# Wider idle matmuls and merged memsets at the start of a sliding-window attention and MLP kernel

## The chip, the cores and the metric

The kernel runs on one core of a Trainium2 chip. The metric is the device time of one execution in microseconds (us); lower is better. TensorE (PE) does matrix products and writes them to PSUM, VectorE (DVE), ScalarE (ACT) and GpSimd (POOL) work on data in SBUF and PSUM, and transfers are issued from GpSimd, ScalarE and SyncE (SP).

## What is computed

Windowed attention (each query sees the keys at most 32 positions away) over 8 batches of 8 heads, 576 tokens and 64 dimensions, and then an MLP with a squared ReLU on the 4608 tokens that come out.

```python
def _attn_ref(q, k, v):                      # each (8, 8, 576, 64)
    scores = scale * np.matmul(q, k.transpose(0, 1, 3, 2))
    mask = np.abs(pos[:, None] - pos[None, :]) <= 32
    scores = np.where(mask, scores, -1000000000.0)
    scores = scores - np.max(scores, axis=-1, keepdims=True)
    attn = np.exp(scores)
    attn = attn / (np.sum(attn, axis=-1, keepdims=True) + 1e-09)
    return np.matmul(attn, v)

def _moe_ref(x, w_in, w_out):                # x (4608, 512), w_in (512, 2048)
    r = np.maximum(x @ w_in, 0.0)
    return (r * r) @ w_out
```

## The kernel before

Every piece of work is recorded as an operation with its engine, its reads and writes, an estimated duration and a key (`Prog.rec`). A planner (`schedule`, `forward`, `backward`) then simulates the engines and the transfer queues with these estimates, tries several orders, keeps the best, and writes the instructions out engine by engine in that order. Between engines, and between dependent instructions of VectorE or of ScalarE, the kernel waits on semaphores that are worked out from the reads and writes; on TensorE the order alone does it.

A batch has nine chunks of 64 queries. For a chunk, K and Q (token by token in `kraw` and `qraw`) are transposed on TensorE (`tok_turn`, line 490) and copied to `kt` and `qt` (lines 501 and 504); from the second or third batch on most transposes are done by transfers. `scores` multiplies them (line 596), ScalarE takes the exponential and VectorE multiplies by the band mask into `pt` (line 633). `av` multiplies `pt` with V (lines 739 and 740), `evac` divides by the sums (lines 750 and 752) into `xr`, `xturn` transposes that (line 768) and ScalarE copies it to `xt`. For the first two chunks the mask is instead added in PSUM by a matmul of the identity with `neg` (line 580), ahead of the scores, and `pt` comes straight from the exponential.

V lies in `vx`, with two columns of ones beside the 64 of each head, so that the product with `pt` also gives the sums. Odd chunks need V shifted by 64 rows; `vd_half` makes that copy, `vd`, on VectorE (line 542). The MLP follows: `mm1_small` in pieces of 128 tokens at first (line 787), then `mm1_half` (line 810) and `mm1` (line 828), with ReLU on ScalarE and the square on VectorE (line 843) into `gt`, and `mm2` (line 880) with the second weights. MLP work of one tile of 512 tokens is interleaved with the attention of later ones.

Two parts concern this change. First, `fill`: after planning, it goes through TensorE's operations up to the first matmul of the MLP (`self.first`) or 36 us of the plan, and puts idle matmuls into the planned gaps. These multiply a tile of zeros, `zz`, with itself into a PSUM bank, `outp1`, that nobody reads before the MLP writes it (line 411). Each has 128 columns; the planner counts 107 ns for it in the first 6 us of the plan and 54 ns after that. A gap gets as many as fit, times a factor (1.15 early, 0.95 later), and the first matmul of the MLP gets six more ahead of it.

Second, the setup on VectorE, all through `ms` (line 405). `setup_ptz` zeroes four stretches of 64 columns in each of the three parts of `pt` (12 memsets). `setup_rest` is called for both buffers of batch data. It zeroes 32 rows of `vx` at either end of the sequence, sets the columns of ones in the rows beside them and in between (four memsets), and zeroes the 32 columns of padding at either end of `kt`. `setup_masks` builds the identity, `mask` and `neg` on the same engine between them.

Of the kernel before, what the change touches and what calls it, by code (L numbers as in the profile page):

```python
# [11 lines left out]
B_, H_, S_, D_ = 8, 8, 576, 64  # L12
# [7 lines left out]
VS = D_ + 2  # L20
KW = 32 + S_ + 32
LEAD = 12
WARM, COLD, DENSE, SPARSE, EXTRA = 36000, 6000, 1.15, 0.95, 6
# [24 lines left out]
class Prog:  # L48
# [257 lines left out]
    def fill(self, out):  # L306
        at = 1200
        for op in sorted((o for o in out if o.eng == "PE"), key=lambda o: o.start):
            gap = min(op.start, WARM, self.first.start) - at
            one = 107 if at < COLD else 54  # L310
            for k in range(int((gap - 60) * (DENSE if at < COLD else SPARSE) // one) + (EXTRA if op is self.first else 0)):
                w = Op()
                w.eng, w.fn, w.dma, w.deps, w.i = "PE", self.idle, None, {self.idle_on}, op.i
                w.inc, w.val, w.sem, w.start, w.end, w.dur, w.key = False, None, None, min(at + one * k, op.start - 1), 0, one, -99
                out.append(w)
            at = max(at, op.start + op.dur)
        self.ops = sorted(out, key=lambda o: (o.start, o.i))

# [40 lines left out]
class Gen:  # L359
# [47 lines left out]
    def setup_idle(self):  # L407

        self.ms("DVE", ["zz"], self.ZZ[:], 0.0, -1000, 200)
        self.p.idle_on = self.p.ops[-1]  # L410
        self.p.idle = lambda e: e.matmul(self.OUTP[1][:, 0:128], self.ZZ[:, 0:128], self.ZZ[:, 0:128], start=True, stop=True)  # L411

    def setup_masks(self, key):
        self.p.rec("POOL", lambda e: e.iota(self.IOTA[:], [[1, 256]], base=0, channel_multiplier=-1), writes=["iota"],
# [15 lines left out]
                   reads=["iota"], writes=[("mask2", 1)], key=-20, dur=130)  # L430

    def setup_rest(self, i, key):
        for s, r in ((0, 0), (4, 96)):
            self.ms("DVE", [("vxz", i, s)], self.VX[i][r:r + 32, s, :, :], 0.0, key, 160)
        self.ms("DVE", [("vxone", i, 0)], self.VX[i][32:64, 0, :, 64:VS], 1.0, key, 80)
        self.ms("DVE", [("vxone", i, 1)], self.VX[i][64:128, 0, :, 64:VS], 1.0, key, 80)
        self.ms("DVE", [("vxone", i, 2)], self.VX[i][0:96, 4, :, 64:VS], 1.0, key, 80)
        self.ms("DVE", [("vxone", i, 3)], self.VX[i][:, 1:4, :, 64:VS], 1.0, key, 120)
        self.ms("DVE", [("ktpad", i, 0)], self.KT[i][:, :, 0:32], 0.0, key)
        self.ms("DVE", [("ktpad", i, 1)], self.KT[i][:, :, 32 + S_:KW], 0.0, key)  # L440

    def setup_ptz(self, i, key):
        for j in range(4):
            self.ms("DVE", [("ptz", i)], self.PT[:, 768 * i + 192 * j + 64:768 * i + 192 * j + 128], 0.0, key, 70)

    def pieces(self, b):
        return PIECE2 if b >= TB else PIECE if b else PIECE0
# [88 lines left out]
    def vd_half(self, b, s0, s1, key, tie=()):  # L536
        vd, vx = self.VD[b % 2], self.VX[b % 2]
        for lo in range(2):
            dst = vd[64 * lo:64 * lo + 64, s0:s1, :, :].rearrange("p s h d -> p (s h d)")
            src = vx[64 - 64 * lo:128 - 64 * lo, s0 + lo:s1 + lo, :, :].rearrange("p s h d -> p (s h d)")  # L540
            rd = list(tie) + [("vxl", b % 2, s + lo) + u for s in range(s0, s1) for u in ((), (1,))] + [("vxone", b % 2, k) for k in range(4)]
            self.p.rec("DVE", lambda e, d=dst, c=src: e.tensor_copy(d, c), reads=rd,  # L542
                       writes=[("vd", b % 2, s, lo) for s in range(s0, s1)], key=key, dur=80 + 145 * (s1 - s0), att=True)

# [10 lines left out]

    def qk_tags(self, b, c):
        i = b % 2
        rd = [("ktpad", i, 0), ("ktpad", i, 1)]
        for x, (t0, n) in enumerate(self.pieces(b)):
            if t0 < 64 * c + 96:  # L560
                rd.append(("k", i, x))
            if t0 < 64 * c + 64:
                rd.append(("q", i, x))
        return rd
# [83 lines left out]
    def v_tags(self, b, c):  # L648
        i, s = b % 2, c // 2
        if c % 2:  # L650
            return [("vd", i, s, 0), ("vd", i, s, 1)]
        return [("vxl", i, s), ("vxl", i, s, 1)] + [("vxone", i, k) for k in range(4)] + ([("vxz", i, s)] if s in (0, 4) else [])

    def av3(self, n, w):
        b, c = divmod(n, NCH)
# [66 lines left out]
    def av(self, n):  # L722
        b, c = divmod(n, NCH)
        i = b % 2
        s = c // 2
        key = n - LEAD
        vt = self.VX[i][:, s] if c % 2 == 0 else self.VD[i][:, s]
        x = n % 3
        k = self.group[n][1]
        bank = "BD"[n % 2] if n < 8 else "CB"[k] if self.group[n][2] > 1 else "B"  # L730
        tag, avp = "s" + bank, self.BK[bank]
        self.bank[n] = bank

        def f(e):
            for j in range(4):
                ha = 4 * (j // 2) + j % 2
                o = avp[:, VE * j:VE * j + VE]
                a = 768 * x + 192 * (2 * (j % 2) + j // 2)
                e.matmul(o, self.PT[:, a:a + 128], vt[:, ha, 0:VE], start=True, stop=False)
                mm = e.matmul(o, self.PT[:, a + 64:a + 192], vt[:, ha + 2, 0:VE], start=False, stop=True)  # L740
            return mm

        self.p.rec("PE", f, reads=self.v_tags(b, c) + [("pt", x), ("ptz", x)], writes=[tag], key=key, dur=240, att=True)

    def evac(self, n, m, gi, k):
        rs, y = self.RS[n % 4], gi % 4
# [167 lines left out]
    def build(self):  # L914
# [4 lines left out]
        K = -200.0  # L919
        self.setup_idle()  # L920
        self.setup_masks(K - 20)
        self.setup_rest(0, K + 3)
        self.setup_ptz(0, K + 2)
        self.setup_ptz(1, K + 2)
        self.setup_ptz(2, K + 2)
        self.setup_rest(1, -20)
        at = {it: K + 1 + k for k, it in enumerate(ORDER)}
        for d in range(4):
# [4 lines left out]
        for b in range(B_):  # L933
# [24 lines left out]
            for c in range(NCH):  # L958
                n = NCH * b + c
# [33 lines left out]
                if c % 2 and not b:  # L993
                    x = (c + 1) // 2
# [6 lines left out]
                gi, k, m = self.group[n]  # L1001
# [48 lines left out]
```

The softmax here doesn't subtract the row's maximum and nothing guards it: scores larger than these inputs give would overflow.

## Time and profile before

| | us |
|---|---|
| median of 4 runs | 300.65 |
| lowest and highest of them | 300.43, 300.88 |
| the profiled execution | 301.47 |
| its span, first to last instruction | 299.7 |

The profile is of one execution. It gives the busy time of each engine, a timeline, and a chain of waits: from the last instruction back to what released it, and so on to the start. Operations are named by output and input tile and by line, so `outp<-zz` at line 411 is an idle matmul. A matmul's own duration in the profile includes its way through the array, some 0.2 us, in which the next ones already run; the rate is read from the spacing of starts, or from the chain, where each piece ends when the next begins. `(partitions x elements, type)` gives an instruction's shape. Some matmuls can be missing from a trace.

How the page splits the span into 40 slices of 7.5 us shows where each engine is busy, in tenths, and the granted clock of TensorE:

```profile
PE   7799999999999999999999999999999999999996
...
DVE  5875646764988965886569745756477622222200
...
POOL 8999841431524544442434334234410000000000
PEclk9999999999999999999999999999999999999999
DMA  9999999999999999999999999999993110100022
```

The part of the program that the change touches is the first three slices.

### The profile page before, as it was taken

The numbers are of one execution on the slowest core, as the hardware profiler recorded it, in microseconds if no ns is written. First come the engines' busy times: TensorE is split into PE (matmuls) and PEld (weight loads), VectorE is DVE, ScalarE is ACT, GpSimd is POOL, SyncE is SP. The second block draws the span as 40 slices with busy tenths as digits, with TensorE's granted clock in tenths as the row PEclk, the third lists the DMA queues.
The fourth block names the chain that finished last, engine by engine and source line by source line (L and its number), as shares of the span: only waits on it lengthen the run. The fifth ranks groups of instructions, "written<-read, shape, count | busy, mean of one in ns | idle before, by whom it ended". The sixth has DMA issues, their size and how long they took to land.

```text
span 299.7 us, 7036 instructions
## 1 busy us (share of the span) xinstructions
PE 290.7 (97%) x2754; PEld 171.7 (57%) x2789; DVE 176.3 (59%) x428; ACT 160.2 (53%) x267; POOL 104.8 (35%) x131
## 2 busy tenths in 40 slices
PE   7799999999999999999999999999999999999996
PEld 7699955866767764545445444544444444444445
DVE  5875646764988965886569745756477622222200
ACT  3466633656757665665647554664656443444311
POOL 8999841431524544442434334234410000000000
PEclk9999999999999999999999999999999999999999
DMA  9999999999999999999999999999993110100022
GB/s 155 168 202 170 206 172 194 151 144 196 152 176 160 126 180 161 152 137 181 131 132 137 152 164 130 120 151 147 156 121 76 49 49 35 37 35 36 35 89 89
DMA packets 166817, 39.34 MB, mean 131 GB/s; under 512 B 157824, under 2 KB 162304, under 8 KB 166784
## 3 DMA queue, kind: packets, MB, share of 16 engines
q0 software_dynamic: 113120, 17.90, 89.4%
q1 hardware_dynamic: 46512, 11.15, 25.9%
q10 hardware_dynamic: 7152, 9.83, 10.1%
q8 instruction: 22, 0.36, 0.5%
q14 instruction: 11, 0.09, 0.1%
HBM read 36.70 MB, written 9.44 MB: 154 GB/s over the span
## 4 chain that ended last, share of the span: by engine, by line
PE 92%; DVE 3%; DMA 2%; issue 1%; ACT 0%; ACTq 0%; POOL 0%; DVEq 0%; POOLq 0%
PE outp L880 40%; PE ht L828 27%; PE ht L810 7%; PE ht L787 7%; PE sc L664 3%; PE sc L596 3%; DMA kraw<-in_k_dram 2%; DVE vd L542 1%; PE sc L490 1%; DVE xr L752 1%; PE sc L856 1%; PE outp L856 1%; PE outp L411 1%; PE sc L712 0%; DVE kt L504 0%
## 5 line engine op out<-in xcount | busy, mean ns | idle before, releaser
L880 PE MATMUL outp<-w,gt 128*128 128x512 bf16 x534 | 133.9, 379 | 2.0 <-issue 1.0
L843 DVE TENSOR_TENSOR gt<-rt 128x512 bf16<-128x512 bf16 x144 | 59.6, 419 | 62.8 <-ACT rt L834 53.3
L828 PE MATMUL ht<-xt,w 128*128 128x512 bf16 x375 | 95.8, 379 | 0.6 <-issue 0.2
L834 ACT ACTIVATE rt<-ht 128x512 bf16<-128x512 f32 x96 | 57.3, 599 | 68.9 <-PE ht L828 64.2
L880 PEld LDWEIGHTS outp<-w,gt 128*128 128x128 bf16 x560 | 52.4, 98 | 57.4
L828 PEld LDWEIGHTS ht<-xt,w 128*128 128x128 bf16 x384 | 36.8, 98 | 43.1
L464 POOL DMA_DIRECT2D qraw<-in_q_dram x39 | 34.1, 875 | 49.7 <-PE ht L828 13.2
L464 POOL DMA_DIRECT2D kraw<-in_k_dram x39 | 34.2, 876 | 36.8 <-PE ht L828 17.6
L530 POOL DMA_DIRECT2D vx<-in_v_dram x40 | 35.1, 879 | 29.2 <-PE ht L828 15.7
L624 ACT ACTIVATE e<-sc 128x1024 bf16<-128x1024 f32 (+1 forms) x46 | 35.7, 819 | 8.2 <-PE sc L596 8.2
L887 ACT ACTIVATE oe<-outp 128x512 f32<-128x512 f32 x35 | 20.9, 598 | 22.4 <-PE outp L880 22.4
L688 DVE TENSOR_TENSOR xr<-pf,rs 128x512 bf16<-128x512 f32 (+1 forms) x42 | 27.6, 682 | 0.4
L787 PE MATMUL ht<-xt,w 128*128 128x128 bf16 x384 | 23.8, 219 | 0.0
L810 PE MATMUL ht<-xt,w 128*128 128x256 bf16 x192 | 23.5, 273 | 0.0
L645 DVE TENSOR_TENSOR pt<-e,mask 128x512 bf16<-128x512 bf16 x42 | 17.7, 422 | 8.9 <-ACT e L624 8.8
L787 PEld LDWEIGHTS ht<-xt,w 128*128 128x128 bf16 x384 | 21.8, 98 | 0.4
L681 DVE COPY pf<-sc 128x520 f32<-128x520 f32 x21 | 14.7, 699 | 11.2 <-PE sc L664 11.1
L810 PEld LDWEIGHTS ht<-xt,w 128*128 128x128 bf16 x192 | 18.0, 98 | 3.3
L795 ACT ACTIVATE rt<-ht 128x512 bf16<-128x512 f32 x24 | 14.2, 599 | 9.2 <-PE ht L787 8.8
L816 ACT ACTIVATE rt<-ht 128x512 bf16<-128x512 f32 x24 | 14.4, 600 | 7.1 <-PE ht L810 6.0
L683 DVE TENSOR_TENSOR pf<-pf 64x520 f32<-64x520 f32 x21 | 14.6, 697 | 5.8 <-ACT pf L678 5.0
L678 ACT ACTIVATE pf<-sc 128x520 f32<-128x520 f32 x21 | 12.6, 600 | 7.2 <-PE sc L664 6.8
(81 smaller groups left out, 192.2 us busy)
## 6 DMA issues: line engine op xcount, KB each, us to landing
out_dram<-oe ACTq DMA_DIRECT2D x35, 256.0 KB, 3.1
kraw<-in_k_dram POOLq DMA_DIRECT2D x30, 128.0 KB, 5.3
qraw<-in_q_dram POOLq DMA_DIRECT2D x30, 128.0 KB, 5.5
vx<-in_v_dram POOLq DMA_DIRECT2D x24, 128.0 KB, 5.5
w<-in_moe_w_in_dram POOLq DMA_DIRECT2D x4, 512.0 KB, 10.0
w<-in_moe_w_out_dram POOLq DMA_DIRECT2D x4, 512.0 KB, 16.5
vx<-in_v_dram POOLq DMA_DIRECT2D x16, 96.0 KB, 5.3
xt<-xr SPq DMA_TRANSPOSE x36, 4.6
```

Source lines behind the costliest of these rows:

```text
L464: self.p.rec("POOL", lambda e: e.dma_start(dst, src), writes=[("fraw", b, t, x)], old=[("fraw", b - 2, t, y + (b == 2))], reads=self.pace( ...
L530: self.p.rec("POOL", lambda e: e.dma_start(self.VX[b % 2][r:r + n, s, :, 0:64], self.v[b, :, t0:t0 + n, :].rearrange("h p d -> p h d")), w ...
L624: self.p.rec("ACT", lambda e, d=dst, a=src: e.activation(d, a, ACTF.Exp, scale=0.125), reads=["s" + x for x in name], writes=[("e", h)], k ...
L645: self.p.rec("DVE", lambda e, a=pt, c=ee, d=mb: e.tensor_tensor(a, c, d, ALU.mult), reads=[("e", k // 2), "mask"], writes=[("ptt", k)], ol ...
L688: self.p.rec("DVE", lambda e, w=w, np=np: e.tensor_tensor(bass.AP(self.XR, 512 * (2 * y + w), [[2048, np], [64, 2], [128, 4], [1, 64]]), b ...
L787: mm = e.matmul(ht[:, 128 * (d % 4):128 * (d % 4) + 128], self.W1[:, ft, 128 * d:128 * d + 128], self.XT[:, ft, t0:t0 + 128], start=(ft == ...
L810: mm = e.matmul(ht[:, 256 * (d % 2):256 * (d % 2) + 256], self.W1[:, ft, 128 * d:128 * d + 128], self.XT[:, ft, 64 * s0:64 * s0 + 256], st ...
L828: mm = e.matmul(ht[:], self.W1[:, ft, 128 * d:128 * d + 128], self.XT[:, ft, 512 * T:512 * T + 512], start=(ft == 0), stop=(ft == 3))
L834: self.p.rec("ACT", lambda e: e.activation(rt[:], ht[:], ACTF.Relu), reads=[("ht", k % 2)], writes=[("rt", k % 4)], key=key, dur=560)
L843: self.p.rec("DVE", lambda e: e.tensor_tensor(g, r, r, ALU.mult), reads=[("rt", k % 4)], writes=tags, key=key, dur=430)
L880: mm = e.matmul(op, gt[:, d, 128 * u:128 * u + 128], self.W2[:, d, :], start=(d == 0), stop=(d == 15))
L887: self.p.rec("ACT", lambda e: e.activation(oe[:], op, ACTF.Copy), reads=[tag], writes=[("oe", x % 4)], key=key, dur=560)
```

## The change

`fill` now works out the columns that a gap needs, in steps of 32, and issues them as idle matmuls of up to 512 columns; a rest under 64 columns is dropped. The zeros that are streamed come from one run of 32 elements of `zz`, repeated by a stride of 0. The weights stay the 128 x 128 zeros.

In the setup, the ones of a `vx` buffer are set by one memset over all rows and all five blocks, and the two zero memsets come after it and read its tag, so that they wait for it. The two paddings of `kt` become one memset with a stride between them, and the 12 memsets of `pt` one. The tags that readers wait for shrink with them (`("vxone", b % 2)`, `("ktpad", i)`, `"ptz"`).

```diff
@@ fill
-            for k in range(int((gap - 60) * (DENSE if at < COLD else SPARSE) // one) + (EXTRA if op is self.first else 0)):
+            cols = max(0, int((gap - 60) * (DENSE if at < COLD else SPARSE) / one * 4)) * 32 + (128 * EXTRA if op is self.first else 0)
+            t = at
+            while cols >= 64:
                 w = Op()
-                w.eng, w.fn, w.dma, w.deps, w.i = "PE", self.idle, None, {self.idle_on}, op.i
-                w.inc, w.val, w.sem, w.start, w.end, w.dur, w.key = False, None, None, min(at + one * k, op.start - 1), 0, one, -99
+                n = min(cols, 512)
+                w.eng, w.fn, w.dma, w.deps, w.i = "PE", (lambda e, n=n: self.idle(e, n)), None, {self.idle_on}, op.i
+                w.inc, w.val, w.sem, w.start, w.end, w.dur, w.key = False, None, None, min(t, op.start - 1), 0, one * n // 128, -99
                 out.append(w)
+                t, cols = t + w.dur, cols - n
@@ setup_idle
-        self.p.idle = lambda e: e.matmul(self.OUTP[1][:, 0:128], self.ZZ[:, 0:128], self.ZZ[:, 0:128], start=True, stop=True)
+        self.p.idle = lambda e, n: e.matmul(self.OUTP[1][:, 0:n], self.ZZ[:, 0:128], bass.AP(self.ZZ, 0, [[128, 128], [0, n // 32], [1, 32]]),
+                                            start=True, stop=True)
@@ setup_rest, setup_ptz
+        self.ms("DVE", [("vxone", i)], self.VX[i][:, :, :, 64:VS], 1.0, key, 130)
         for s, r in ((0, 0), (4, 96)):
-            self.ms("DVE", [("vxz", i, s)], self.VX[i][r:r + 32, s, :, :], 0.0, key, 160)
-        self.ms("DVE", [("vxone", i, 0)], self.VX[i][32:64, 0, :, 64:VS], 1.0, key, 80)
-        self.ms("DVE", [("vxone", i, 1)], self.VX[i][64:128, 0, :, 64:VS], 1.0, key, 80)
-        self.ms("DVE", [("vxone", i, 2)], self.VX[i][0:96, 4, :, 64:VS], 1.0, key, 80)
-        self.ms("DVE", [("vxone", i, 3)], self.VX[i][:, 1:4, :, 64:VS], 1.0, key, 120)
-        self.ms("DVE", [("ktpad", i, 0)], self.KT[i][:, :, 0:32], 0.0, key)
-        self.ms("DVE", [("ktpad", i, 1)], self.KT[i][:, :, 32 + S_:KW], 0.0, key)
-
-    def setup_ptz(self, i, key):
-        for j in range(4):
-            self.ms("DVE", [("ptz", i)], self.PT[:, 768 * i + 192 * j + 64:768 * i + 192 * j + 128], 0.0, key, 70)
+            self.p.rec("DVE", lambda e, s=s, r=r: e.memset(self.VX[i][r:r + 32, s, :, :], 0.0), reads=[("vxone", i)],
+                       writes=[("vxz", i, s)], key=key, dur=160)
+        self.ms("DVE", [("ktpad", i)], bass.AP(self.KT[i], 0, [[4 * KW, 128], [KW, 4], [32 + S_, 2], [1, 32]]), 0.0, key, 160)
+
+    def setup_ptz(self, key):
+        self.ms("DVE", ["ptz"], bass.AP(self.PT, 64, [[2304, 128], [192, 12], [1, 64]]), 0.0, key, 300)
...
-        self.setup_ptz(0, K + 2)
-        self.setup_ptz(1, K + 2)
-        self.setup_ptz(2, K + 2)
+        self.setup_ptz(K + 2)
```

## The prediction

> **What bounds the kernel now.** I read the page's span, its busy lines and its chain first, to see which engine sets the end.
>
> ```profile
> span 299.7 us, 7036 instructions
> ...
> PE 290.7 (97%) x2754; PEld 171.7 (57%) x2789; DVE 176.3 (59%) x428; ACT 160.2 (53%) x267; POOL 104.8 (35%) x131
> ...
> PE 92%; DVE 3%; DMA 2%; issue 1%; ACT 0%; ACTq 0%; POOL 0%; DVEq 0%; POOLq 0%
> ```
>
> TensorE is busy for 97% of the span and holds 92% of the chain that ended last. So whatever moves the start of its dense work moves the end by as much. All idle matmuls (line 411) and all memsets of the diff stand in the first 20 us, so the second view is that chain over the first 40 us (start, duration, what).
>
> ```profile
> 1.35 5.88 DMA kraw<-in_k_dram
> ...
> 7.28 0.53 PE sc L490 x8
> ...
> 8.44 0.70 DVE kt L504
> ...
> 16.56 0.40 PE outp L768 x4
> 16.96 0.61 PE outp L411 x11
> ...
> 18.50 0.89 PE outp L411 x16
> 19.39 0.89 PE ht L787 x16
> ```
>
> Four stretches follow. Until 7.24 us a transfer of K holds the chain. From 7.28 to 8.4 TensorE works on what it brought. From 8.44 to 16.51 it is VectorE, copy after copy. From 16.56 it is TensorE for good, and there two groups of idle matmuls lie on the chain itself: 11 before the P·V matmuls, 16 before the first matmul of the MLP (line 787). Third, TensorE's timeline, for what lies ahead of 7.28.
>
> ```profile
> 2.77 2.07 PE L411 MATMUL outp<-zz 128*128 128x128 bf16 x18
> ...
> 5.47 0.78 PE L411 MATMUL outp<-zz 128*128 128x128 bf16 x11
> ...
> 7.28 0.29 PE L490 MATMUL sc<-identw,kraw 64*128 64x64 bf16 x4 [0.68 <-DMA kraw<-in_k_dram]
> ```
>
> The bracket is what to see: TensorE stood idle for 0.68 us before that transfer. Up to 0.68 us of delay ahead of it costs nothing. Fourth, VectorE's groups of the first 37 us by shape (busy us, mean ns).
>
> ```profile
> L542 DVE COPY vd<-vx 64x528 bf16<-64x528 bf16 x8 | 4.5, 566 | 0.2
> ...
> L405 DVE MEMSET vx<- 32x264 uint32 x4 | 1.1, 278 | 0.2
> L405 DVE MEMSET pt<- 128x32 uint32 x12 | 0.7, 85 | 0.0
> ```
>
> **Does the order change?** The listings of the two built programs have the same order on ScalarE, GpSimd and SyncE, every instruction in its place. On TensorE only the idle matmuls differ, on VectorE only the memsets of the setup. No transfer is moved past another, and the plan for the other 280 us is the same. So the sum has only local terms.
>
> **The idle matmuls.** Before there are 103 of 128 columns, 13,184 columns in all. After there are 13,760 in 31 instructions (counted in the listing): the groups of 13, 18, 2, 11, 10, 2, 8, 6, 2, 4, 11 and 16 become 1952, 2048, 320, 1440, 1376, 288, 1024, 832, 288, 576, 1504 and 2048 columns, and one of 64 is new. In time:
>
> - Slow-clock prices. The 18 that began at 2.77 were followed by the next work at 4.68, 1.91/18 = 0.106 us for 128 columns. Group one grows by 288 columns, +0.24 us; group two shrinks by 256, -0.21. The next two grow by 64 and 32 columns, at the fast price below +0.04. Together some +0.07 us before 7.28. The work that covers it is the K transfer: 0.68 us of idle time becomes 0.61. Without that cover it would cost its 0.07.
> - Groups between 8.44 and 16.51. They grow by 96, 32, 0, 64, 32, 64 and 64 columns, +0.01 to +0.04 us each. VectorE's chain covers them: TensorE waits 1.61 us for xr at 13.48 and 0.32 at 16.56. Without the cover the sum is 352 columns, 352/128 x 0.056 = 0.15 us.
> - The two groups on the chain. The 16 took 0.89 us, 0.0557 for 128 columns. A 512-column matmul on contiguous data takes 0.216 (line 880, four in 0.86 us in the chain). The 11 become 1504 columns: 1504/512 x 0.216 = 0.63 against 0.61, +0.02. The 16 become four of 512: 0.86 against 0.89, -0.03. Sum -0.01 us.
>
> **What no row shows: runs of 32.** The new idle matmul streams one run of 32 elements again and again (stride 0), where the old one read 128 in a row. Nearest is line 580, which streams 256 columns in runs of 64 by stride 0: its two took 0.42 us on the slow clock (2.35 to 2.77), 0.105 for 128 columns, the full rate. That is the lower bound, a cost of nothing. Upper bound: each run costs as much as the smallest separate matmul in the trace, 0.03 us (lines 739 and 740, 0.03 each in the chain). On the chain 1504 + 2048 columns are 111 runs: 3.33 us against 1.50, +1.8 us. I take nothing, since line 580 is the same form with runs only twice as long.
>
> **The memsets.** From the two rows above a memset costs 85 ns for 32 elements and 278 for 264: (278 - 85)/232 = 0.83 ns an element. Twelve of pt become one of 384 elements, 85 + 352 x 0.83 = 0.38 us. The timeline has the first four spaced 0.04 us apart, so twelve took some 0.49: -0.1. For each vx buffer six become three, and four of kt become two of 128 elements, 0.16 us each. The setup, done at 5.10 us before, ends near 4 us, some 1.1 us earlier. This buys nothing: what follows it on VectorE, the copy of kt at 5.22, waits for the transposes that TensorE issues at 4.68 (4.75 after). One order matters: a vx zero memset now stands ahead of neg, and TensorE's second real work (line 580, 2.35 us) reads neg. In the timeline neg ended at 2.02 + 0.18 = 2.20; with 278 ns in place of 85, some 0.05 more for the other two, it ends near 2.45. TensorE's first idle group now holds it until 0.98 (its start) + 1952/128 x 0.107 = 2.61 us. That is the cover, and behind it stands the 0.68 again; without both it would cost 0.25 us. Two new waits of VectorE on its own memset (zeros after ones) hold mask work and kt memsets behind them, all done a microsecond before use.
>
> **A lock between VectorE and GpSimd.** The copies vd<-vx are where the long VectorE stretch has play. In the chain the seven on it take 0.70, 0.72, 0.75, 0.29, 0.60, 0.33 and 0.85 us for one shape: 4.24 us, 2.2 more than seven at 0.29. GpSimd is busy throughout, issuing transfers 0.86 us apart. Memsets don't seem to disturb it: its issues at 3.59 and 4.47, with memsets running, are 0.88 apart. So I expect GpSimd's phase unchanged, and since VectorE's chain starts when a transfer lands, its phase too: 0.
>
> The Trainium skill has the mechanism (SBUF — State Buffer, Who interferes with whom): copies in a two-port mode and GpSimd exclude one another for a whole instruction, while a memset with no SBUF input stays out of it. By that rule the term is 0 as well; by the row alone it could be anything down to -2.2. Speaking against the change is TensorE: Matmul & The Clock Gate (What's actually happening): the clock opens after about 3.4 us of busy time, counted in a free-running window, not in matmuls. By it longer idle matmuls bring nothing, and if the window fell differently, the opening would move in both kernels alike.
>
> In this trace the spacing went from 0.106 us (the 18) to 0.056 (the 11 from 5.47: 0.78 us less the 0.22 that one takes, over 10). Should it open only after 7.28, the 1760 idle columns from 4.68 would take 0.7 us more, and 0.6 of that is covered. The old kernel, with 1664 such columns, would lose 0.65, so the difference is under 0.1 us.
>
> **The sum.** Profiled execution: 301.47 us, of which 299.7 are span and 1.8 lie around it. Change: 0 (before 7.28) + 0 (to 16.51) - 0.01 (the two groups) + 0 (setup) = -0.01, so 301.46 for it. The profiled execution is 0.82 above the median of the runs, 300.65, so in a run without a profile I say 300.6 us.
>
> **Rivals.**
>
> - *Short runs are slow* (8%). Place: the idle groups at 16.96 and 18.50. Price: up to +1.8 us, so 302.4. It decides from +0.6 us, 0.0054 us more for each of the 111 runs. For it: no row has runs of 32. Against it: line 580 at full rate.
> - *The lock falls otherwise*. If half of the 2.2 us goes, 299.5 us (17%); if as much is added, 301.7 (13%). For it: copies of one shape between 0.29 and 0.85 us, all on the chain. Against it: GpSimd's order and pace don't change, and the four runs before, whose transfers land a little differently each time, lie within 0.45 us.
> - *The K transfer lands earlier* (7%), with VectorE's setup a microsecond shorter while GpSimd issues it. Price: at most the 0.68 us that TensorE stands waiting for it, so 299.9. Against it: its issue, 1.35 to 2.16 us, runs beside VectorE work that is much the same in both.
> - *It doesn't do what it says*, within the forecast: idle columns are the same to 4%, so a clock that opens at the same time was to be expected.
>
> **How the numbers follow.** No change has 55%, with its own range 300.2 to 301.1 (the spread of the four runs, and 0.2 about it). Faster is 17 + 7 = 24%, slower 8 + 13 = 21%. What a measurement of this kernel can tell from no change is about 0.2%, 0.6 us. For the range I go into both sides until about a tenth is left out at each end: 299.7 to 301.5.
>
> **What would show it.** Right: line 411 at 0.216 us for 512 columns on the fast clock, first MLP matmul near 19.2 us, wait for kraw near 0.6, neg before 2.6. Wrong: idle matmuls of over 0.25 us on the fast clock; vd copies whose sum leaves 4.2 by more than 0.6; a kraw landing that isn't near 7.24; a first MLP matmul that moves by over 0.6 us with the end following it.

## The result and the profile after

| | before | after |
|---|---|---|
| median, us | 300.71 (62 runs, 300.36 to 301.81) | 301.48 (44 runs, 300.46 to 304.89) |
| ratio | | 1.0033, 95% interval 1.0023 to 1.0042 |
| the profiled execution, us | 301.47 | 302.38 |
| its span, us | 299.7 | 300.6 |

The change makes the kernel 0.33% slower, 0.8 to 1.0 us by the medians and the ratio. The lowest times are nearly the same; what changed is how often they are reached. Of the 62 runs before, the lower half lies between 300.36 and 300.7; of the 44 after, only eight are below 300.8.

First the page of the changed kernel: span, busy lines, chain.

```profile
span 300.6 us, 6872 instructions
...
PE 290.9 (97%) x2682; PEld 167.4 (56%) x2717; DVE 174.8 (58%) x409; ACT 160.1 (53%) x267; POOL 105.4 (35%) x131
...
PE 88%; DVE 5%; DMA 4%; issue 2%; ACT 1%; POOL 0%; DVEq 0%; POOLq 0%; ACTq 0%
```

TensorE is as busy as before, with 72 matmuls and 72 weight loads fewer. But the chain no longer stays with it: DMA has 4% where it had 2%. To see where, I set the start of each of TensorE's 2,686 weight loads that are not idle work beside the same one of the kernel before (the order is the same). After minus before, in us:

| weight load for | start before | start after | difference |
|---|---|---|---|
| first real matmuls that wait for K (line 490) | 7.28 | 7.35 | +0.07 |
| second xr transpose (line 768) | 16.56 | 15.44 | -1.12 |
| xr transpose near 23 us (line 768) | 22.91 | 21.80 | -1.11 |
| line 828, first | 110.90 | 110.72 | -0.19 |
| line 828, near 139 us | 139.08 | 140.05 | +0.97 |
| the last | | | +0.96 |

So the part that the change touches became 1.1 us shorter in this execution, and 2 us were lost far behind it, at two places above all: 0.8 us by the first matmul of line 828, at 110.72, and 1.15 us near 139. At the first the changed kernel has this wait:

```profile
110.75 1.02 PE L829 MATMUL ht<-xt,w 128*128 128x512 bf16 x4 [0.66 <-issue]
```

Six profiles of the experiments lose 0.2 to 0.6 us there as well, by the same comparison against the run with 231 idle matmuls, which has neither wait. One of the six has the old idle matmuls, and no block of instructions (explained below) was fetched in it between 100.0 and 113.4 us. So the first wait isn't shown to have the cause of the second. Here is the chain of waits of the changed kernel around 139 us:

```profile
133.47 0.72 DVE xr L689 x2
134.19 5.81 DMA xt<-xr
140.01 0.05 issue
140.05 1.90 PE ht L829 x8
```

TensorE (line 829 is line 828 of the kernel before) stands still until a transfer has landed that transposes `xr` into `xt`. Now SyncE's own timeline at that place, before and after (start, duration of the issue):

```profile
134.37 1.19 SPq L699 DMA_TRANSPOSE xt<-xr  x1
```

```profile
134.19 2.19 SPq L700 DMA_TRANSPOSE xt<-xr  x1
```

It is the same issue at nearly the same time, but it took a microsecond longer. In the kernel before, line 828 did not wait:

```profile
139.10 1.89 PE L828 MATMUL ht<-xt,w 128*128 128x512 bf16 x8
```

The DMA queues around that issue show what else was there, before (134.3 to 136.4 us) and after (134 to 136.4 us):

```profile
q0 software_dynamic: 1040, 0.13, 98.0%
q1 hardware_dynamic: 387, 0.09, 26.4%
```

```profile
q0 software_dynamic: 1014, 0.13, 96.7%
q1 hardware_dynamic: 370, 0.09, 31.9%
q8 instruction: 1, 0.02, 4.9%
```

One packet of 16 KB on q8 fell on the issue: a block of instructions. It began at 134.1 us and took 1.9. The same answers have the transfer landing 5.8 us after its issue, against 4.4 before. In the kernel before, such blocks came at 127.5 and at 140.2 us.

### The profile page after: what moved, and what is told of

Read it like the earlier page. It is cut to its first block, busy times and chain, and to the rows that moved or that the text cites. A ratio compares the mean times of both kernels' runs of the same rounds, so it can differ in the third digit from the quotient of the medians.

```text
span 300.6 us, 6872 instructions
## 1 busy us (share of the span) xinstructions
PE 290.9 (97%) x2682; PEld 167.4 (56%) x2717; DVE 174.8 (58%) x409; ACT 160.1 (53%) x267; POOL 105.4 (35%) x131
## 4 chain that ended last, share of the span: by engine, by line
PE 88%; DVE 5%; DMA 4%; issue 2%; ACT 1%; POOL 0%; DVEq 0%; POOLq 0%; ACTq 0%
PE outp L881 37%; PE ht L829 27%; PE ht L788 7%; PE ht L811 6%; PE sc L597 3%; PE sc L665 3%; DMA kraw<-in_k_dram 2%; DMA xt<-xr 2%; DVE vd L543 1%; PE sc L491 1%; PE outp L415 1%; DVE pf L684 1%; DVE xr L689 1%; DVE gt L844 1%; PE sc L857 1%
## 5 line engine op out<-in xcount | busy, mean ns | idle before, releaser
L465 POOL DMA_DIRECT2D qraw<-in_q_dram x39 | 33.4, 858 | 49.2 <-PE ht L829 20.4
L465 POOL DMA_DIRECT2D kraw<-in_k_dram x39 | 33.4, 858 | 38.6 <-PE ht L829 20.2
```

What stands on the lines that cost most here:

```text
L465: self.p.rec("POOL", lambda e: e.dma_start(dst, src), writes=[("fraw", b, t, x)], old=[("fraw", b - 2, t, y + (b == 2))], reads=self.pace( ...
```

## The experiments

Each was timed beside the kernel before on the same chip. I named the theories in the expectations: A (an earlier start makes TensorE run into its transfers), A' (the wide idle matmuls cost by themselves), B (the places at which TensorE's instructions are fetched), C (the memsets).

**The two halves of the change.** The idle matmuls alone: the diff of `fill` and `setup_idle`, nothing of `setup_rest` and `setup_ptz`.

> The kernel before with the wide idle matmuls alone; its memsets are the old 16. Theory A (the change starts the dense matmuls some 1.1 us earlier, as in the profile after, and TensorE then runs into transposing transfers xt<-xr that it used to meet when they were done): if the idle matmuls bring the earlier start, the first MLP matmul stands near 18.1 us, line 828 waits for xt<-xr, and the median is 301.2 to 301.8; if not, 19.2 us and 300.6 to 300.8. Rival B (fewer TensorE instructions move the fetches of its instructions against other transfers): 301.2 to 301.8 whatever the start. Rival C (the memsets do it): 300.6 to 300.8.

Measured: 302.0 us, ratio 1.0040 (1.0025 to 1.0055). The memsets alone: the rest of the diff.

> The kernel before with the merged memsets alone; its idle matmuls have 128 columns. Theory A: the time goes with the start; first MLP matmul near 18.1 us and 301.2 to 301.8, or near 19.2 us and 300.6 to 300.8. Rival B: 300.6 to 300.8. Rival C: 301.2 to 301.8.

Measured: 300.94 us, ratio 1.0008 (0.9996 to 1.0020). The memsets are not told from no change, so C falls; the idle matmuls carry the loss, as far as can be told. In both profiles the first MLP matmul stands near 18.2 us, so the early start is not what tells them apart, and A falls with it. The profile of the idle matmuls alone has the same picture as the full change, SyncE's issue first, then TensorE:

```profile
133.61 1.78 SPq L704 DMA_TRANSPOSE xt<-xr  x1
```

```profile
139.80 1.89 PE L833 MATMUL ht<-xt,w 128*128 128x512 bf16 x8 [1.30 <-issue]
```

A block fetch began at 133.2 us there and took 1.7. (The releaser is named "issue" here, but the transfer landed 6.1 us after its issue, at 139.71, just ahead of this matmul.)

**Later and earlier starts.** The changed kernel with a later start:

```diff
-WARM, COLD, DENSE, SPARSE, EXTRA = 36000, 6000, 1.15, 0.95, 6
+WARM, COLD, DENSE, SPARSE, EXTRA = 36000, 6000, 1.15, 0.95, 26
```

> The changed kernel with 20 x 128 more idle columns ahead of the first MLP matmul, 1.1 us. Theory A: the dense work starts where the kernel before starts it, the waits for xt<-xr go, and the time falls to 300.5 to 300.9 though 1.1 us of idle work was added. Rivals B and C: the 1.1 us is added to what there was, 302 to 302.7.

Measured: 302.61 us, ratio 1.0055 (1.0037 to 1.0073). And the kernel before with an earlier one:

```diff
         for op in sorted((o for o in out if o.eng == "PE"), key=lambda o: o.start):
+            if self.first.start - 3500 < op.start <= self.first.start:
+                at = max(at, op.start + op.dur)
+                continue
```

> The kernel before without the last three groups of idle matmuls (4, 11 and 16), so that its dense work starts up to 1.5 us earlier; memsets and idle width as before. Theory A: earlier start, no gain at the end, and waits for xt<-xr: 301 to 302, with a wide spread. Rivals B and C: the earlier start is passed on, 299.2 to 300.0.

Measured: 300.67 us, ratio 0.9999 (0.9988 to 1.0009). By the median the late start brought nothing back, its 1.1 us came on top. Its profile, though, has no wait at 139; the issue there was a short one:

```profile
135.72 1.19 SPq L700 DMA_TRANSPOSE xt<-xr  x1
```

What makes that execution long (302.76 us) is its start: the second xr transpose stands at 16.56, as in the kernel before, and with the added columns the first MLP matmul at 20.30. So this run alone does not decide against A; the memsets alone, which start early and lose nothing that can be told, do, and so do two runs below with early starts.

The early start missed both expectations, without the loss that A wanted and without the gain of the others. In its profile the first MLP matmul stands at 17.36, 0.8 us ahead of the 18.2 of the profiles above, and waits behind it leave 0.4 us of that by 30 us. I had also overlooked that it has 72 idle matmuls and not 103, so under B its fetches stand elsewhere too; a later run mends that.

**Count against width.** TensorE fetches its instructions in blocks. The traces show it in the number of blocks on q8: 22 with 103 idle matmuls, 21 with 31, and 23 with 231 (a run below). Before there are 5,578 matmuls and weight loads (2,789 of each; 35 matmuls are missing from the trace), so a block holds some 254 of them. The Trainium skill (Runtime: NRT & Kernel Launch, Instruction fetch mechanics) says that instructions come in 16 KiB blocks of 256, and calls the cost of crossing a boundary "mostly hidden". The size agrees with the counts. What TensorE itself loses at a boundary no run here separates; the 2.19 us above are a delay of another engine, SyncE, by TensorE's fetch.

If the place of a block is what matters, then the number of TensorE instructions modulo 256 must set the time, and the width of an idle matmul must not. Narrow and wide, each with both counts, makes a square. Old width, new place: 56 of the 103 idle matmuls are issued as two of 64 columns.

```diff
+        halves = 56
...
                 out.append(w)
+                if halves:
+                    halves -= 1
+                    w.fn = lambda e: self.idle(e, 64)
+                    v = Op()
...
+                    out.append(v)
```

> The kernel before; 56 of its 103 idle matmuls are split into two of 64 columns, so the columns, the memsets and the order stay and TensorE has 112 instructions more. Its instructions are fetched in blocks of 16 KB (22 in the profile before, for some 5,580 instructions: 256 a block), so after 112 more the fetches fall at the same places of the program as with the 144 fewer of the changed kernel (256 apart). Theory B (a fetch that falls on an xt<-xr transfer delays it, and line 828 waits): a fetch near 133 to 135 us, the xt<-xr issue there 1.7 to 2.2 us instead of 1.2, line 828 late by 1 us or more near 139, and a median of 301.2 to 302. Theory A' (wide idle matmuls themselves do it): 300.6 to 300.8.

Measured: 301.36 us, ratio 1.0028 (1.0012 to 1.0044). New width where it is on the chain, old count:

```diff
-                n = min(cols, 512)
+                n = min(cols, 512 if op.start > self.first.start - 2600 else 96 if at < COLD else 128)
```

> The changed kernel with its last two idle groups 512 wide as they are, and the earlier ones cut into 96 and 128 columns, so that there are 103 idle matmuls again, as many as before. Theory B: fetches where the kernel before has them (near 127 and 140 us), no wait at 139, and 300.6 to 301.0. Theory A': wide idle matmuls still stand on the chain, 301.2 to 302.

Measured: 301.17 us, ratio 1.0008 (0.9993 to 1.0024). The median lies above what B had (300.6 to 301.0) and just below what A' had. But the memsets alone, which differ from this kernel in the width and a little in the number of the idle columns, have the same ratio, 1.0008. So the ratio goes with the count, not with the width:

| | 103 idle matmuls | 31, 32 or 159 |
|---|---|---|
| 128 columns or fewer | 1 (before), 1.0008 (with the new memsets) | 1.0028 |
| 512 columns on the chain | 1.0008 | 1.0033, 1.0040 |

(31 and 159 are 128 apart, so 256 instructions.) The profile of the kernel with 159 shows the wait, SyncE first, then TensorE:

```profile
133.36 1.60 SPq L707 DMA_TRANSPOSE xt<-xr  x1
```

```profile
139.12 1.90 PE L836 MATMUL ht<-xt,w 128*128 128x512 bf16 x8 [0.86 <-DMA xt<-xr]
```

Its block began at 133.3 us. In the profile with 103 wide and narrow ones the blocks began at 126.3 and 139.2 us, the issue at 133.38 took 1.19, and line 829 began at 138.11, with no wait.

**Other places.** Idle matmuls of up to 256 columns:

```diff
-                n = min(cols, 512)
+                n = min(cols, 256)
```

> The changed kernel with idle matmuls of up to 256 columns: 58 of them, 90 TensorE instructions fewer than before in place of 144. Theory B: the fetch of 134 us comes 54 instructions sooner in the program, near 131, off the xt<-xr issue at 134; 300.5 to 301.0 unless it meets another one that TensorE waits for. Theory A': between the two kernels or like the changed one, 301.0 to 301.8.

Measured: 301.73 us, ratio 1.0024 (1.0007 to 1.0040), 58 idle matmuls. The expected place was wrong: the block began at 133.2 us, not near 131, and took 1.0, so it ended 0.2 us after the issue of 134.04 had begun; that issue took 1.19, and this one execution (301.04 us) had no wait at 139, but lost 0.6 us near 110. The runs spread from 300.41 to 302.80. Why the place moves by less than the count says is not shown. Two more counts, with 28 in place of 56 halves, and with 88 idle matmuls (`128` in place of `96 if at < COLD else 128`):

> The kernel before with 28 of its idle matmuls cut in two (131 in place of 103; columns, memsets and order as before): fetches 56 instructions sooner in the program, so near 123 to 125 and 136 to 139 us. Theory B: no xt<-xr issue that TensorE waits for stands there, 300.5 to 300.9; if the fetch near 138 falls on the issue of 138.3 and line 828 waits after 142, 301.2 or more. Theory A': 300.6 to 300.8.

> The changed kernel with 128-column idle matmuls except in the last two groups: 88 of them, 30 TensorE instructions fewer than before. Theory B: the fetches come some 2 us later than before, near 129 and 141, off the issue of 134; 300.4 to 300.9. Theory A': 301.0 to 301.8.

Measured: 301.07 us, 1.0008 (0.9998 to 1.0018), and 301.51 us, 1.0019 (1.0006 to 1.0032). The first is some 0.2 us above what was expected and not told from no change. The second missed, and so did the 256 columns: both lie where A' had them, and what speaks against A' is the square and the profiles of the pair below. Neither profile of the two has the wait at 139. B says that the place of the blocks matters; it did not forecast what these other places cost.

**Without the victim.** Both kernels with every `xr` transposed on TensorE (`NPE = 72` in place of 18), which gives the two one common order:

> The kernel before with every xr transposed on TensorE and copied by ScalarE: no xt<-xr transfer is left for a fetch to fall on. The order is planned anew and TensorE has 18 more groups of transposes, so it is compared with the next kernel, which has the same order. Theory B: no line 787, 810 or 828 waits on a transfer of xt; 303 to 312 us.

> The same with the wide idle matmuls and the merged memsets, in the same order otherwise. Theory B: the victim is gone, so the two differ by under 0.4 us, and the spread of this one is no wider than the other's. Theory A' (something in the wide idle matmuls or in the memsets costs by itself): this one is 0.8 to 1.4 us slower, as the changed kernel is against the one before.

Measured: 314.26 us (six runs, 313.65 to 315.75) and 315.19 us (six, 314.56 to 316.59), against the kernel before 1.0450 (1.0423 to 1.0477) and 1.0474 (1.0448 to 1.0500). The level was misjudged. The medians differ by 0.93 us, as A' had it and not B, but the intervals overlap, so the pair does not tell. Its profiles (315.73 and 315.68 us) say more: compared weight load by weight load, from 25 us to the end the second is never later than the first. So in these two executions the wide idle matmuls and the new memsets cost nothing, with 142 instructions fewer and no transfer of `xt` to meet. Why the medians differ stays open; 60 transposing transfers, of `kt` and `qt`, are left in both.

**A whole block more.** The kernel before with 31 of its idle matmuls cut in four and 35 in two, so 231 in place of 103: 256 instructions more, the same columns.

> The kernel before with idle matmuls cut in two and in four, 231 in place of 103: 256 TensorE instructions more, one whole block, with the same columns, memsets and order. Theory B by the place of the block ends: fetches after 40 us where the kernel before has them (near 127 and 140 us), 300.5 to 300.9. Rival B' (any other number of idle matmuls than 103 costs, or more instructions cost by their number): more than the 301.36 of the kernel with 159, 301.4 to 302.5.

Measured: 300.50 us, ratio 1.0003 (0.9993 to 1.0013). This is the strongest of the runs: 112 instructions more cost 0.28%, 256 more cost nothing that can be told, so neither the number as such nor a count other than 103 is what costs. Its first MLP matmul stands at 18.19, early, and without a loss. In its profile the blocks began at 126.8 and 139.6 us, and this is SyncE's timeline, then TensorE's:

```profile
133.33 1.19 SPq L708 DMA_TRANSPOSE xt<-xr  x1
```

```profile
138.06 1.89 PE L837 MATMUL ht<-xt,w 128*128 128x512 bf16 x8
```

**An attempt at a better kernel.** The early start again, with 31 of the remaining 72 idle matmuls cut in two, so 103:

> The kernel before without the last three groups of idle matmuls, as in the earlier run that started its dense work early, but with 31 of the others cut in two, so that there are 103 again. Theory B (the number of TensorE instructions, taken modulo the 256 of a fetched block, sets which transfers a fetch falls on): fetches where the kernel before has them, the earlier start is passed on, 299.6 to 300.3. If only the start counted, it would be like the early run before it, 300.67. If idle matmuls just ahead of the dense part are needed for something else: over 300.9.

Measured: 300.32 us (12 runs, 300.04 to 301.88), ratio 0.9994 (0.9981 to 1.0006). The median is 0.4 us below that of the kernel before, beside it, and just outside what B had; the interval holds no change. The profiled execution was its slowest, 301.88 us, and shows a second victim, in the chain:

```profile
78.49 8.18 DMA xt<-xr
86.67 0.05 issue
86.71 1.05 PE ht L821 x8
```

A transposing transfer issued at 78.49 landed only at 86.67, and TensorE waited 1.31 us. A block had been fetched at 80.3, while that transfer was under way and on the next issue of `xt<-xr`, at 80.22, which took 1.74 us. That the block delayed the first of the two is not shown.

**All profiles together.** The 15 profiled executions, with the two kernels themselves, hold 1,368 transposing issues of SyncE. Of 196 that overlap a 16 KB block, 119 took over 1.5 us (61%). Of the other 1,172, 18 did (1.5%). A longer issue has more chance to meet a block, but not by so much. At the one issue near 134 us, the two kernels and the 11 experiments that kept the order compare directly. In three profiles (the change, the idle matmuls alone, 159 idle matmuls) a block lies on it, it took 1.60 to 2.19 us, the transfer landed 5.7 to 6.1 us after its issue, and TensorE waited at 139. In the other ten it took 1.19 or 1.20, the landing came after 3.8 to 4.4, and there was no wait. In two of those ten (the late start and the 256 columns) a block touched the issue as well, without effect.

## Why the prediction was wrong

- **Idle matmuls: right.** The timeline of the changed kernel has the four before the MLP in their place:

```profile
17.26 1.02 PE L415 MATMUL outp<-zz 128*128 128x512 bf16 x4
...
18.12 1.06 PE L788 MATMUL ht<-xt,w 128*128 128x128 bf16 x16
```

  They hold 0.86 us, 0.215 each, as the sum had it. Runs of 32 elements cost nothing; that rival falls.
- **Memsets: right.** In the profile `neg` began at 2.19 us and was done at 2.29, before TensorE wanted it at 2.59, and the setup ended at 4.04. The cover was larger than forecast: TensorE waited 1.09 us for the K transfer in place of 0.61, since its second idle group, 2,048 columns, ran from 3.02 to 4.43: 0.088 us for 128 columns in place of 0.106. The prediction puts such spacings down to the clock; the granted clock of the profile reads 1.00 from 1 to 7 us in both kernels and does not show it.

```profile
7.35 0.29 PE L491 MATMUL sc<-identw,kraw 64*128 64x64 bf16 x4 [1.09 <-DMA kraw<-in_k_dram]
```

- **The lock between VectorE and GpSimd: no term of the change, but misread.** The copies, by the groups of the first 37 us of the changed kernel:

```profile
L543 DVE COPY vd<-vx 64x528 bf16<-64x528 bf16 x8 | 3.4, 429 | 0.2
```

  That is 3.4 us against 4.5, and it is the 1.1 us by which the start was earlier (the first MLP matmul at 18.12, not near 19.2). It is not due to the change: of the 11 experiments that kept the order, 10 have the second xr transpose near 15.4 us in their profile, among them those with the old memsets and idle matmuls of the old width; one has it at 16.56, as the kernel before had in its own. The execution from which I predicted was a long one, 0.8 us above the median, and I took its copies for the kernel's.
- **The step that failed** is this sentence: "No transfer is moved past another, and the plan for the other 280 us is the same. So the sum has only local terms." I had counted that 103 instructions become 31, but priced their columns only. What the runs showed in its place: 144 TensorE instructions fewer move every later instruction block against the rest of the program, and where a block lands on the issue of a transposing transfer that TensorE waits for, it can cost over 1 us (near 139 us 1.15 us in the changed kernel, 1.45 with the idle matmuls alone and 1.04 with 159 narrow ones, by the comparison of starts just ahead of the wait and behind it). The kernel as a whole lost 0.8 to 1.0 us by the median and the ratio.
- **The range** held the time, 301.48 against an upper end of 301.5, but by luck: from other causes than those it was made of. None of the rivals had a place behind 20 us: "the plan for the other 280 us is the same" had kept the steady part of the kernel out of sight.

What stays open: by what path a block slows SyncE's issue. The traces don't tell on which of the 16 DMA engines a packet ran, and not every overlap costs. The loss in single runs is spread over several places, of which the profiles show some (139 us, 110 us, in one run 87 us, in two between 20 and 28 us); that the wait at 139 us makes up all of the difference in the medians is not shown. Nor is it shown how often each kernel has the long start, which costs as much (1.0 to 1.1 us): with one profile of each, that the changed kernel has it more often can't be ruled out, though the three profiles with the wait at 139 all start early.

## What to carry to other kernels

Where transfers that an engine waits for have little slack, the number of instructions of that engine can be a parameter itself: here it set where instruction blocks were fetched. After an edit that changes a count, compare the fetch times and the durations of the issues beside them, and try the same edit with the count made up (here modulo 256) before judging it. And before predicting from one profiled execution, set its time against the median: if it is 0.8 us above, find the stretch that is long in it.

## What I had not expected of the hardware

- A fetch of 16 KB of instructions takes 0.9 to 2.5 us here while the other queues are busy, and transposing issues that it overlaps went from 1.2 us to between 1.5 and 3.2 in six of ten cases.
- Copies of one shape from SBUF to SBUF on VectorE took 0.29 to 0.85 us while GpSimd issued transfers, and kernels with the same order of work on both engines came out 1.1 us apart by 16 us from their start.
